# A warm-up of the matmul engine, later diagonals, and the last attention slot of the first batch turned by blocks, in a fused threshold attention and MLP kernel

## The chip, the cores and the metric

The kernel runs on one core of one Trainium2 chip. The metric is the device time of the whole kernel in microseconds (us). Before the change it took 1442.96 us, the median of three runs (1442.68 to 1445.76). The profile shown here is of one execution, whose span is 1443.0 us.

## The reference

Two blocks follow one another. The first is an attention with a threshold, for batch 8, 8 heads, 576 positions and head width 64; the second is a layer norm, a two-layer MLP with a residual, of width 512 and hidden width 2048.

```python
scores = (q @ k.T) / 8                       # per batch and head: 576 x 576
thresh = max(scores, axis=-1) - tau
scores = where(scores >= thresh, scores, -1e9)
attn = exp(scores - max(scores)); attn = attn / (sum(attn) + 1e-9)
x = attn @ v                                 # heads side by side: (8, 576, 512)
xn = (x - mean(x)) / sqrt(var(x) + 1e-6) * g_ln
out = x + relu(xn @ w_ch1) @ w_ch2
```

All inputs are float32 but the two weight matrices, which arrive as float64; the kernel converts them itself.

## The kernel before, in words

**Slots.** The attention is cut into 72 slots, nine for each of the eight batches; n counts all slots from 0, s is the slot within its batch. A slot handles a pair of heads (a unit) with 256 of its query rows: slots s = 0 to 3 take the first 256 rows of the four pairs, s = 5 to 8 the next 256, and s = 4 takes what is left over of all four. The loop over the slots is lines 749 to 811. A slot runs: score products on PE (line 384), row maxima on DVE (398) and thresholds on POOL (402), exponentials on ACT (409), masking and row sums on DVE (416), the reciprocal of the sums (420). The weights then have to be turned (transposed) before they can be multiplied by v.

**Two ways to turn the weights.** In batch 0 (slots n = 0 to 8) the turn is done on PE: ACT makes four diagonal matrices that hold the reciprocals (427), and in the next slot PE multiplies each 128 x 128 piece of the weights by a diagonal (lines 453, 468; recorded as line 100 tile `tp`, and line 468 tile `tr`); ACT copies the results out of PSUM into `em` and `rest` (462, 477). From batch 1 on the turn is done by blocks: POOL scales the weights by the reciprocals (429), DVE transposes 32 x 32 blocks into a tile `et` (494), four transfers write `et` to a scratch `scr` in DRAM (500), and in the next slot two transfers read it back in the turned order into `em` and `rest` (509, 510). For this way the queries must have been turned in another order of columns, which `by_blocks` also decides (338). In both ways the product with v (538) of slot n is issued in the last quarter of slot n + 1 once the first batch's early slots are past.

**MLP steps between.** A group is half a batch (288 tokens), 16 groups in all. A generator (`ffn_steps`, 632) yields the MLP's products one at a time, and `second_part` (702) places a number of them in each of four quarters of a slot. The first layer's product for one of 16 hidden blocks is 16 PE instructions (each float32 product is two halves and is run in two passes), then ACT applies the relu (649) into `hidden`. The second layer's are 64 PE instructions for each of four output blocks; DVE multiplies the result by the inverse deviation (596) and POOL adds x (597), DVE transposes (602), and four transfers store it. PSUM gives two buffers (tag `ff`) to all of these, so a product waits for the reader of the product two before it.

**Weight conversion.** The weights come in 32 chunks of 512 KB (16 of the first layer, then 16 of the second). `fetch` (229) issues a transfer on the SP queue into a free room; rooms are lent by `w2_sb`, `hidden`, `et`, an x buffer and a staging tile, each up to a given chunk (211 to 215). At a later `tick` (306) a chunk is begun (DVE 263 and 267, ACT 271 and 275), carried (POOL 281), masked (DVE 290), and for the first layer scaled by `g_ln` (ACT 303). `fetch` stands at two places of a slot (762 and 802). The last chunks are converted in slots n = 8 and 9.

**What orders the work.** Every engine and the SP queue run their instructions in the order in which the program writes them: `manual_schedule` is set, and no scheduler moves anything. SP issues nearly all transfers, and a transfer whose wait is not met holds up all behind it. In the built program the transfers take eight semaphores in rotation, so the issue of one also waits until the transfer eight before it has landed. `load_qk` (102) loads queries and keys of the next unit as soon as the turn of the present one (321) has freed their single buffers. `run(n, i)` (691) runs what was put off to quarter i of slot n (i = -1: right after the scores).

Of the kernel before, what the change touches and what calls it, by code (L numbers as in the profile page):

```python
# [18 lines left out]
def kernel(  # L19
# [31 lines left out]
    nc = tc.nc  # L51
# [72 lines left out]
    def load_v(u):  # L124
# [9 lines left out]
        values_in[u] = (vt, vr)  # L134

    ctx.enter_context(tc.manual_schedule())
    nc.sync.dma_start(
        out=tau_sb, in_=bass.AP(tensor=tau.tensor, offset=tau.offset, ap=[[0, 128], [1, 1]])
    )
# [6 lines left out]
    load_v(0)  # L146
    make_identity(nc, ident)
    nc.vector.memset(eps_sb, 1e-6)
    nc.vector.memset(avg_sb, 1.0 / DM)

# [13 lines left out]
    class Weights:  # L166
# [13 lines left out]
        def __init__(self):  # L180
            self.chunks = [
                (w1_sb[i][:, c : c + WC], w_ch1[i * 128 : (i + 1) * 128, c : c + WC], i)
                for c in range(0, DF, WC)
                for i in range(NK)
            ] + [
                (
                    w2_sb[:, m, d : d + 4].rearrange("p d c -> p (d c)"),
                    w_ch2[d * 128 : (d + 4) * 128, m * 128 : (m + 1) * 128].rearrange(
                        "(d p) c -> p d c", p=128
                    ),  # L190
                    None,
                )
                for m in range(NK)
                for d in range(0, ND, 4)
            ]
            self.n1 = NK * (DF // WC)
            self.fetched = self.begun = self.carried = self.masked = self.ended = 0
            self.raw, self.made, self.due, self.ticks = {}, {}, [], 2
            flat = lambda t: t.rearrange("p a b -> p (a b)")

            x_room = ffn.tile([128, NK, TOK], F32, tag="x", bufs=3, name="x_room")
            stage = consts.tile([128, 8, WC], F32, name="stage")
            et = att.tile([128, NB, 128], F32, tag="et", bufs=1, name="et0")

            n1 = self.n1
            self.free = []
            for t, n, before in (  # L210
                (w2_sb.rearrange("p m d c -> p (m d) c"), ND // 2, lambda p: n1 + 2 * p),
                (hidden, 4, lambda p: 10),
                (et, 2, lambda p: 2 * n1),
                (x_room, 1, lambda p: 2 * n1),
                (stage, 4, lambda p: 2 * n1),
            ):
                for p in range(n):
                    self.free.append((before(p), -1, flat(t)[:, p * 2 * WC : (p + 1) * 2 * WC]))
# [95 lines left out]
            if self.begun < self.fetched:  # L314
                self.begin()

    def by_blocks(u):

        return units[u][0] > 0

    def turn(u):

        q_in, k_in = loaded.pop(u)
        qT = att.tile([128, 2, QH], F32, tag="qT", bufs=4, name="qT")
        kT = att.tile([128, S], F32, tag="kT", bufs=4, name="kT")  # L330
        ql = q_last[u % HP]
        nc.gpsimd.tensor_scalar(
            out=q_in, in0=q_in, scalar1=scl_sb, scalar2=1.0, op0=ALU.mult, op1=ALU.mult
        )
        nc.vector.transpose(kT, k_in.rearrange("p n c -> p (n c)"))
        for s in range(2):
            part = q_in[:, 9 * s : 9 * s + 8]
            if by_blocks(u):
                nc.vector.transpose(
                    qT[:, s].rearrange("p (j a c) -> p a j c", j=2, a=4),  # L340
                    part.rearrange("p (a j) c -> p a j c", j=2),
                )
            else:
                nc.vector.transpose(qT[:, s], part.rearrange("p n c -> p (n c)"))  # L344
        nc.vector.transpose(
            ql.rearrange("p (t c) -> p t c", t=2),
            q_in.rearrange("p (t n) c -> p t n c", t=2)[:, :, 8],
        )
        turned[u] = (qT, kT, ql)
# [61 lines left out]
    def weights(es, thr, divide):  # L411
# [6 lines left out]
                op0=ALU.is_ge, op1=ALU.mult, accum_out=den[:, i : i + 1],  # L418
            )
        nc.vector.reciprocal(den, den)  # L420
        diags = []
        for i in range(4):
            if not divide:
                if i % 2 == 0:
                    two = ffn.tile([128, TOK], F32, tag="o", bufs=6, name="diag")
                diags.append(two[:, i % 2 * 128 : i % 2 * 128 + 128])
                nc.scalar.mul(diags[i], ident, den[:, i : i + 1])
                continue
            nc.gpsimd.tensor_scalar(  # L429
                out=es[:, i], in0=es[:, i], scalar1=den[:, i : i + 1], scalar2=1.0,  # L430
                op0=ALU.mult, op1=ALU.mult,
            )
        return diags


# [255 lines left out]
    def run(n, i):  # L691
        for fn, args in later_calls.pop((n, i), ()):
            fn(*args)
# [55 lines left out]
    for n in range(NS):  # L749
# [8 lines left out]
        run(n, -1)  # L758
        rest = exponentials()
        es, thr = next(rest)  # L760
        run(n, 0)
        conversion.fetch(2)
        run_all(stores)
        second_part(n, 0)
        next(rest, None)
# [8 lines left out]
        run(n, 1)  # L774
        second_part(n, 1)
        tick(2)
        blocks_go = by_blocks(b * HP)
        diags = weights(es, thr, blocks_go)
        run_all(aside)
        run_all(stores)  # L780
        tick(3)
        run(n, 2)
        second_part(n, 2)
        tick(4)
        box = []
        if blocks_go:
# [12 lines left out]
        if s in (HP, 2 * HP):  # L799
            group_ready(2 * b + (s > HP))  # L800
        run_all(aside)
        conversion.fetch(2)
        tick(5)
        run(n, 3)
        if b == 0 and s < HP - 2:
# [43 lines left out]
```

## Time and profile before

| What | us |
|---|---|
| span | 1443.0 |
| PE busy | 1389.0 (96%) |
| DVE busy | 871.8 (60%) |
| ACT busy | 422.2 (29%) |
| POOL busy | 439.1 (30%) |
| PE busy in the first 100 us | 68.4 |
| PE busy in 100 to 200 us | 92.8 |
| PE busy in 300 to 1400 us | 1091.8 of 1100 |

The page's second part shows the busy tenths of each engine in 40 slices of 36 us; the third row of interest is the granted PE clock. Its fourth part is the chain of work that ended last. The timeline of an engine lists its instructions in order of time, merged where alike: start, duration, engine, line, operation, tile written and tiles read, and in brackets the idle time before and what ended it. Times are counted from the start of the span. A slot is found in it by its score products (line 384) on PE: n = 0 at 10.0 us, n = 1 at 21.5, n = 6 at 87.4, n = 7 at 119.9, n = 8 at 142.2, n = 9 at 164.6, n = 10 at 191.6, n = 11 at 212.0.

### The profile page before, as it was taken

Reading aid. Unit: us, or ns where it says so; the run is one execution under the profiler, and the core shown is the slowest. Engines: PE = TensorE matmul, PEld = TensorE weight load, DVE = VectorE, ACT = ScalarE, POOL = GpSimd, SP = SyncE. Lnnn points to the kernel's source line nnn. Section 1 sums busy time; section 2 is a strip of 40 time slices with the busy share of each in tenths; the row PEclk is TensorE's granted clock in tenths of the full one; section 3 lists DMA queues with packets and bytes.
Section 4 is the critical chain, followed back from the end, with each engine's and each line's share of the span. In section 5 each row is a group of like instructions: output and inputs, shape, how many; then the busy total and the mean of one; then the engine's idle time right before and its main releaser. Section 6 shows DMA issues by size and latency. Waiting matters only on the chain.

```text
span 1443.0 us, 29649 instructions
## 1 busy us (share of the span) xinstructions
PE 1389.0 (96%) x12168; PEld 859.7 (60%) x12168; DVE 871.8 (60%) x1492; ACT 422.2 (29%) x818; POOL 439.1 (30%) x681
## 2 busy tenths in 40 slices
PE   5879999999999999999999999999999999999998
PEld 3655666655556565655556555565556555565664
DVE  5998857556565666566655565556665566656111
ACT  3887513132221313132221312223132322213020
POOL 2444332333323233232322333232332323222100
PEclk8999999999999999999999999999999999999999
DMA  9622466657845677557855577555775578555301
GB/s 226 168 73 83 90 137 157 172 148 162 176 133 145 148 173 173 145 131 171 183 150 145 146 160 167 140 144 143 176 167 143 136 170 185 139 144 137 79 6 17
DMA packets 466840, 205.12 MB, mean 142 GB/s; under 512 B 275024, under 2 KB 428368, under 8 KB 466704
## 3 DMA queue, kind: packets, MB, share of 16 engines
q1 hardware_dynamic: 461936, 202.64, 58.4%
q8 instruction: 95, 1.56, 0.5%
q10 hardware_dynamic: 4736, 0.59, 0.4%
q14 instruction: 41, 0.34, 0.1%
q0 software_dynamic: 32, 0.00, 0.0%
HBM read 119.41 MB, written 83.76 MB: 141 GB/s over the span
## 4 chain that ended last, share of the span: by engine, by line
PE 85%; DVE 4%; DMA 4%; SPq 3%; ACT 2%; issue 1%; POOL 0%; POOLq 0%; DVEq 0%; ACTq 0%
PE p L100 64%; PE sc L538 10%; PE sc L384 9%; SPq L115 2%; DMA em<-scr 1%; DVE e L416 1%; PE tp L100 1%; DVE neg L398 1%; DMA v_in<-in_v_dram 1%; ACT e L409 1%; DMA rest<-scr 0%; DMA scr<-et 0%; PE mean L100 0%; DVE w L263 0%; SPq L500 0%
## 5 line engine op out<-in xcount | busy, mean ns | idle before, releaser
L100 PE MATMUL p<-xc,w 128*64 128x288 f32 x4096 | 515.2, 407 | 7.4 <-ACT hidden L649 5.9
L100 PE MATMUL p<-hidden,w 128*64 128x288 f32 x4096 | 513.7, 407 | 0.0
L100 PEld LDWEIGHTS p<-xc,w 128*64 128x64 f32 x4096 | 294.9, 137 | 211.9 <-ACT hidden L649 12.6
L100 PEld LDWEIGHTS p<-hidden,w 128*64 128x64 f32 x4096 | 297.9, 137 | 196.5 <-issue 9.3
L398 DVE TENSOR_REDUCE neg<-sc 128x2 f32<-128x1152 f32 x144 | 188.7, 1352 | 252.2 <-PE sc L384 252.2
L409 ACT ACTIVATE e<-sc,neg 128x576 f32<-128x576 f32 x288 | 194.5, 742 | 296.5 <-DVE neg L398 290.1
L429 POOL TENSOR_SCALAR e<-e,den 128x576 f32<-128x576 f32 x252 | 187.9, 763 | 239.6 <-DVE den L420 239.5
L416 DVE SCALAR_TENSOR_TENSOR e<-sc,thr,e 128x576 f32<-128x576 f32 x288 | 219.0, 810 | 23.7 <-ACT e L409 23.7
L494 DVE STREAM_TRANSPOSE et<-e 128x1152 f32<-128x1152 f32 x112 | 153.6, 1375 | 77.3 <-POOL e L429 57.1
L649 ACT ACTIVATE hidden<-p 128x288 f32<-128x288 f32 x256 | 105.7, 413 | 292.0 <-PE p L100 290.6
L384 PE MATMUL sc<-kT,qT 64*128 64x384 f32 (+3 forms) x1024 | 150.6, 425 | 20.0 <-DVE qT L344 10.0
L402 POOL TENSOR_SCALAR thr<-neg,low_sb 128x2 f32<-128x2 f32 x144 | 41.6, 289 | 387.4 <-DVE neg L398 382.5
L384 PEld LDWEIGHTS sc<-kT,qT 64*128 64x128 f32 x1024 | 94.2, 191 | 77.5 <-issue 27.0
L538 PE MATMUL sc<-em,v_in 128*64 128x256 f32 (+1 forms) x1408 | 131.3, 330 | 6.0 <-DMA em<-scr 2.2
L538 PEld LDWEIGHTS sc<-em,v_in 128*64 128x64 f32 x1408 | 86.9, 137 | 45.8 <-DVE et L494 7.0
L555 ACT COPY x<-sc 128x256 f32<-128x256 f32 x60 | 22.4, 373 | 286.4 <-PE sc L538 284.4
L596 DVE TENSOR_TENSOR o<-p,rb 128x288 f32<-128x288 f32 x64 | 28.4, 443 | 127.9 <-PE p L100 127.9
L597 POOL TENSOR_TENSOR o<-o,x 128x288 f32<-128x288 f32 x64 | 51.0, 797 | 115.4 <-DVE o L596 114.0
L564 POOL TENSOR_TENSOR sum<-sum,x 128x256 f32<-128x256 f32 (+1 forms) x64 | 32.8, 512 | 97.6 <-ACT x L555 95.1
L655 POOL TENSOR_TENSOR sq<-sq 128x288 f32<-128x288 f32 x48 | 38.8, 808 | 44.0 <-ACT sq L653 41.5
L538 PE MATMUL sc<-rest,v_rest 128*64 128x256 f32 (+1 forms) x352 | 44.7, 329 | 0.0
L100 PE MATMUL tp<-diag,e 128*64 128x128 f32 x576 | 35.5, 278 | 6.6 <-ACT em L462 5.3
(130 smaller groups left out, 701.2 us busy)
## 6 DMA issues: line engine op xcount, KB each, us to landing
scr<-et SPq DMA_DIRECT2D x252, 288.0 KB, 4.6
em<-scr SPq DMA_DIRECT2D x63, 1024.0 KB, 5.9
out_dram<-ot SPq DMA_DIRECT2D x256, 36.0 KB, 4.4
q_in<-in_q_dram SPq DMA_DIRECT2D x124, 72.0 KB, 3.8
k_in<-in_k_dram SPq DMA_DIRECT2D x120, 72.0 KB, 2.8
v_in<-in_v_dram SPq DMA_DIRECT2D x64, 128.0 KB, 4.4
rest<-scr SPq DMA_DIRECT2D x63, 128.0 KB, 6.0
w<-in_moe_w_ch_dram SPq DMA_DIRECT2D x10, 512.0 KB, 6.0
```

What stands on the lines that cost most here:

```text
L100: nc.tensor.matmul(out[r], lhsT=lhsT[:, r], rhs=rhs, **flags)
L384: nc.tensor.matmul(sc[h][64 * i : 64 * i + 64 if s == HP else 128, at : at + n], lhsT=ql[r] if s == HP else qT[r, half, j * 128 : (j + 1) ...
L398: nc.vector.tensor_reduce(out=neg[:, i], in_=pairs[h], axis=AXL.X, op=ALU.max, negate=True,)
L402: nc.gpsimd.tensor_scalar(out=thr[:, i], in0=neg[:, i], scalar1=-1.0, scalar2=low_sb, op0=ALU.mult, op1=ALU.add,)
L409: nc.scalar.activation(es[:, i], blocks[i], func=AF.Exp, bias=neg[:, i : i + 1])
L416: nc.vector.scalar_tensor_tensor(out=es[:, i], in0=blocks[i], scalar=thr[:, i : i + 1], in1=es[:, i], op0=ALU.is_ge, op1=ALU.mult, accum_o ...
L429: nc.gpsimd.tensor_scalar(out=es[:, i], in0=es[:, i], scalar1=den[:, i : i + 1], scalar2=1.0, op0=ALU.mult, op1=ALU.mult,)
L494: nc.vector.transpose(et[:, :, 64 * h : 64 * h + 64].rearrange("p n (j c) -> p j n c", j=2), es[:, 2 * h : 2 * h + 2].rearrange("p j (n c) ...
L538: nc.tensor.matmul(dst[64 * h : 64 * h + 64], lhsT=vt[:, c, h, :] if c < J else vr[:, h, :], rhs=pick(em[:, c] if c < J else er, hp, h), s ...
L597: nc.gpsimd.tensor_tensor(out=o, in0=o, in1=groups[g][:, m], op=ALU.add)
L649: nc.scalar.activation(hidden[:, d], p1, func=AF.Relu)
L655: nc.gpsimd.tensor_tensor(out=sq[:, 0], in0=sq[:, 0], in1=sq[:, c], op=ALU.add)
```

## The change

Four edits are made together.

1. **Warm-up.** The tile `avg_sb`, a constant, is filled first of all on DVE, and PE runs 20 products of it with itself (40 halves of 128 columns) into a PSUM tile that nobody reads, before the first scores. This is to have the PE clock up when the first scores come.
2. **Diagonals later.** For slots n = 5, 6 and 7 the four diagonals on ACT are made after the third quarter's MLP steps, and not before them. This is to keep them out of the way of the relu.
3. **Slot n = 8 by blocks.** The last slot of batch 0 is turned by blocks and not on PE; the second half of the queries of unit 3 is turned accordingly. This takes the 32 halves into `tp` and the 4 products into `tr` off PE. The `et` tile is lent to the conversion only up to chunk 26 (before: 31), so that it is free for this.
4. **Fetches ahead.** Both calls of `fetch` are moved up in the slot, so that chunk transfers stand on the SP queue ahead of the transfers of turned weights: the first before `run(n, 0)`, which reads `scr` back, the second before `turn_blocks`, which writes it.

```diff
+    nc.vector.memset(avg_sb, 1.0 / DM)
+    warm = ps_ff.tile([128, 128], F32, tag="ff", name="warm")
+    for _ in range(20):
+        product(warm, lhsT=avg_sb, rhs=avg_sb, start=True, stop=True)
     nc.sync.dma_start(
...
-                (et, 2, lambda p: 2 * n1),
+                (et, 2, lambda p: 2 * n1 - 5),
...
-    def by_blocks(u):
-        return units[u][0] > 0
+    def by_blocks(n):
+        return n >= 2 * HP
...
-            if by_blocks(u):
+            if by_blocks(SLOTS * (u // HP) + u % HP + s * (HP + 1)):
...
+    def diagonals(den):
+        diags = []
+        for i in range(4):
+            if i % 2 == 0:
+                two = ffn.tile([128, TOK], F32, tag="o", bufs=6, name="diag")
+            diags.append(two[:, i % 2 * 128 : i % 2 * 128 + 128])
+            nc.scalar.mul(diags[i], ident, den[:, i : i + 1])
         return diags
...
         es, thr = next(rest)
+        conversion.fetch(2)
         run(n, 0)
-        conversion.fetch(2)
         run_all(stores)
...
-        blocks_go = by_blocks(b * HP)
-        diags = weights(es, thr, blocks_go)
+        blocks_go = by_blocks(n)
+        den = weights(es, thr, blocks_go)
+        if n <= HP:
+            diags = diagonals(den)
         run_all(aside)
         run_all(stores)
         tick(3)
         run(n, 2)
         second_part(n, 2)
+        if HP < n < 2 * HP:
+            diags = diagonals(den)
+        conversion.fetch(2)
         tick(4)
...
         run_all(aside)
-        conversion.fetch(2)
         tick(5)
```

In the built program the order on PE is the same as before but for the 40 added halves at the start and the 36 of slot 8 (32 into `tp`, 4 into `tr`) that are gone. Beside the turn itself, the other engines' order differs in the conversion: which rooms the chunks use, and when the last ones are fetched and begun. Before, chunks 27 and 28 (counted from 0) are fetched by the first call in slot 8, 29 and 30 by the second, and 31 by the first in slot 9. After, chunk 27 is fetched by the first call in slot 8, 28 and 29 by the second, right ahead of slot 8's `scr` transfers, chunk 30 by the first call in slot 9, right ahead of the read of `scr`, and chunk 31 by the second in slot 9, behind that read, the next query and key loads and four stores. On DVE chunk 28 is begun right ahead of the transposes into `et` of slot 8, and chunk 31 right ahead of those of slot 9. One chunk's mask (290) moves from slot 9 to slot 10, ahead of the subtraction of the mean (579) there.

## Prediction

> **What bounds the kernel now.** I first read the busy tenths. PE is full from about 115 us on, and only before that is there anything to win by waiting less; DVE is full in the slices before.
>
> ```profile
> PE   5879999999999999999999999999999999999998
> DVE  5998857556565666566655565556665566656111
> PEclk8999999999999999999999999999999999999999
> PE 85%; DVE 4%; DMA 4%; SPq 3%; ACT 2%; issue 1%; POOL 0%; POOLq 0%; DVEq 0%; ACTq 0%
> ```
>
> The last line is the chain that ended last: 85% of it is PE. So time is gained in two ways: PE instructions taken out once PE is full, and the first 115 us made shorter. Then I read the timelines around each edit. The start, PE, then DVE, then the SP queue:
>
> ```profile
> 10.04 4.21 PE L384 MATMUL sc<-kT,qT 64*128 64x384 f32 x16 [10.04 <-DVE qT L344]
> 21.50 5.68 PE L384 MATMUL sc<-kT,qT 64*128 64x384 f32 x16 [7.24 <-DVE e L416]
> ...
> 41.03 0.78 DVE L335 STREAM_TRANSPOSE kT<-k_in 128x576 f32<-128x576 f32 x1
> ...
> 33.80 4.79 SPq L115 DMA_DIRECT2D k_in<-in_k_dram  x4
> ```
>
> The first scores take 4.21 us, in slot 7 and later 2.21 for the same 16 instructions. The keys of unit 3 are issued until 38.6 and turned at 41.03. Slot 6, PE and ACT:
>
> ```profile
> 111.73 1.68 PE L100 MATMUL p<-xc,w 128*64 128x288 f32 x12 [2.76 <-ACT hidden L649]
> ...
> 108.39 1.28 ACT L427 ACTIVATE diag<-ident,den 128x128 f32<-128x128 f32 x4
> 109.56 0.72 ACT L303 ACTIVATE w<-w,g_sb 128x512 f32<-128x512 f32 x1
> 111.27 0.70 ACT L649 ACTIVATE hidden<-p 128x288 f32<-128x288 f32 x2
> ```
>
> PE waits 2.76 us for a relu, and ACT, busy without a gap, has the diagonals ahead of it. The turn of slot 8 on PE, and the place where PE next leans on DVE:
>
> ```profile
> 166.76 1.09 PE L100 MATMUL tp<-diag,e 128*64 128x128 f32 x16
> 174.80 11.80 PE L100 MATMUL p<-hidden,w 128*64 128x288 f32 x95
> 203.91 2.16 PE L100 MATMUL p<-xc,w 128*64 128x288 f32 x16 [0.73 <-DVE o L596]
> ...
> 193.91 2.62 DVE L398 TENSOR_REDUCE neg<-sc 128x2 f32<-128x1152 f32 x2 [2.70 <-PE sc L384]
> ...
> 185.61 3.74 SPq L500 DMA_DIRECT2D scr<-et  x4
> 193.93 0.41 SPq L509 DMA_DIRECT2D em<-scr  x1
> ```
>
> The turn costs 174.80 - 166.76 = 8.04 us, of it some 3.5 waiting for ACT's copies. From the write of `scr` to the issue of its read pass 8.32 us.
>
> [...]
>
> **Part 1, warm-up.** [...] DMA is full (the table by stretches gives it shares of 1.02, 1.00 and 0.97 in 10 to 20, 20 to 40 and 40 to 60 us), and unit 3's keys must land before the turn at 41.03. Their issue ends at 38.6, and landing takes 2.4 to 3.1 us from issue by the page's group of transfers: 41.0 to 41.7, or a little earlier for the pieces issued before. So that turn has no slack on its transfers. Earlier turns of units 1 and 2 free the buffers earlier, but an issue also waits for the transfer eight before it, and those are paced by bandwidth. I take 0.8 (0.4 for the POOL and DMA wait behind it and 0.4 for the landing); bounds 0 and 2.0. After that DVE is full until slot 6 and passes on what it got.
>
> **Part 2, diagonals.** In slot 6 the relu comes 1.19 us earlier (the group takes 1.28, starts 1.17 ahead of the next), so PE gains 1.2. The diagonals then lie behind the relu; ACT ends that stretch at 115.6 as before, and the next relu at 116.10 still comes before PE needs it (111.73 - 1.2 = 110.5, then 12 passes, the values' 2.2 and 20 passes: 116.6). In slot 5 no MLP runs, in slot 7 PE did not wait for the relu: 0, hidden behind ACT's conversion and behind 5.74 us of products. Bounds 0 and 1.2; I take 1.2.
>
> **Part 3 and 4, slot 8.** Times in this part are those of before (all is shifted by parts 1 and 2 alike). PE loses 8.04 us of work after 166.8. POOL gains 2.9 (four scalings, as at 203.70), ACT loses its copies; both have room. But DVE and SP get a new order.
> - DVE in slot 8 has one chunk less ahead of the masking, so the masking ends near 158.3 and not 160.3. Then it must begin chunk 28, whose transfer is issued at 157.97 (behind the key loads) and lands 4.0 us later, at 162.0: DVE waits. `et` of slot 8 is then made from 163.1 to 165.9 (2.74).
> - `scr` is written from 165.9; its read is issued 8.3 us later at 174.2 and lands 6.0 later (the group of `em` transfers), at 180.2. PE wants it at 186.28 - 8.04 = 178.2: PE waits 2.0.
> - Chunk 30, issued behind the `scr` writes and the values near 172.2, lands near 176.8; DVE waits for it ahead of slot 9's masking, which ends at 181.6 and not 179.95. This costs PE nothing: the scores of slot 10, which need that PSUM, come at 185.
> - Chunk 31 stands behind the read, the loads of unit 6 and a store. The third key load is the eighth transfer after the read, so it waits for 180.2; two key loads (1.2) and four stores (2.0) later, near 183.5, chunk 31 is issued and lands 4.0 to 5.0 us later, at 188.0.
> - DVE begins chunk 31 ahead of `et` of slot 9. Queued behind it are: that `et` (so slot 9's own turn), a store's transpose, the release of a PSUM buffer (596) for which PE's mean waits, and the maxima of slot 10. From 188.0: 1.1 + 2.75 + 0.43 + 0.45, and the maxima start at 192.7, not at 193.91. From there to the release that PE awaits at 203.91 pass 10.0 us, plus 0.68 for the mask that moved into slot 10: 203.4. And slot 9's `et`, done at 191.85, has its `em` landed at 191.85 + 8.3 + 6.0 = 206.2, where PE wants it at 205.9.
> So of the 8.04 us nothing is left at 206: +0.3 to +0.4. The gain is turned into a wait for the last chunk. Behind 206 PE is full and keeps what shift there is.
>
> Sum: -0.8 - 1.2 + 0.4 = -1.6, from 1442.96: 1441.4.
>
> **Rivals.**
> - *The turn pays.* The last chunks land in time, or DVE's wait lies in slack: PE loses 8.04, waits 2.0 for slot 8's `em`, and pays 0.7 for the moved mask: -5.3. With -0.8 and -1.2: -7.3, 1435.7. For it: chunk transfers waited hardly ever before (0.35 us at 163.56). Against it: they were issued a slot earlier then, and chunk 31 needs 181 for this, when SP still holds the key loads back.
> - *The wait costs more than the turn.* Chunk 30's 512 KB ahead of `em` delays it by 1.7 (512 KB at some 300 GB/s, a fast slice of the DMA row between 140 and 240 us), chunk 31 needs 5.0, and line 263 takes 1.5 and not 0.4, as it does beside POOL at 144.43: 190.7 + 1.1, so +4.2; and with nothing from parts 1 and 2 (the relu meets the next wait), 1447.2. For it: each is seen in the trace. Against it: all must come together.
> - *The start pays in full*: 2.0 from the warm-up, all else as forecast: -2.8, 1440.2; its chance is part of my forecast's.
>
> **How the numbers follow.** Chances: my forecast 0.50 (of it 0.08 below 1440.1), the turn pays 0.32, it costs more 0.18. 0.2% is 2.9 us: faster is below 1440.1, slower above 1445.8. So faster 0.40, same 0.42, slower 0.18. The range reaches to both rivals: 1435 to 1447.
>
> **What would show it.** Slot 0's scores in 2.2 us and slot 1's still slow; unit 3's keys turned at 40 to 41; the relu wait in slot 6 at 1.6; no `tp` rows in slot 9; DVE idle some 2 us in slot 8, and 3 and 5 in slot 9, ahead of the first step of a chunk (line 267 after), for a weight transfer; PE waiting for `em` and for the PSUM release (line 603 after). I am wrong if the DVE waits for chunks 28, 30 and 31 are missing (then 1436), or if unit 3's keys land 2 us earlier.

## The result and the profile after

The changed kernel takes 1458.82 us (median of 6 runs, 1452.38 to 1463.99); the kernel before, run beside it, 1445.18 us. The ratio is 1.0092 with a 95% interval of 1.0064 to 1.0121: it is slower by 13.6 us. The forecast was 1441.4 us, with a range of 1435 to 1447: it was wrong in size and in sign.

The busy tenths and the chain that ended last, from the page of the changed kernel:

```profile
PE   6879989999999999999999999999999999999998
DVE  5899756566665666656665565656665566655211
PEclk8999999999999999999999999999999999999999
PE 78%; DVE 6%; DMA 6%; SPq 4%; ACT 2%; issue 2%; POOL 1%; POOLq 0%; DVEq 0%; ACTq 0%
```

PE's row has an 8 in the sixth slice (182 to 219 us), where before it had nines, and PE's share of the chain fell from 85% to 78%. DMA, DVE and SP took its place. To see where that happened, put the starts of the slots (first score products on PE) of both traces side by side, after minus before in us:

| slot | 1 | 2 | 3 | 6 | 7 | 8 | 9 | 10 | 11 | 12 | 18 | 36 | 71 |
|---|---|---|---|---|---|---|---|---|---|---|---|---|---|
| shift | -2.0 | -0.6 | +1.9 | +1.4 | -0.2 | -0.4 | -0.4 | +0.7 | +4.9 | +9.7 | +9.5 | +11.5 | +15.9 |

There are two losses: 4 us between slots 1 and 3, and 10 us in slots 9 to 11. (Behind slot 12 a trace drifts by some us, here down to +9.5 in slot 18 and up to +15.9 in slot 71, as single reads of `em` come late, by up to 2.7 us, and single stretches run at a slower clock, here 3.41 us at half clock from 902.74; the medians of the runs decide, the shifts only say where.)

**The start**, the timelines of PE and of DVE, and below them the turn of unit 2's keys in the kernel before:

```profile
1.06 6.51 PE L100 MATMUL warm<-avg_sb 128*64 128x128 f32 x80 [1.06 <-DVE eps_sb L153]
10.04 2.21 PE L388 MATMUL sc<-kT,qT 64*128 64x384 f32 x16 [2.47 <-DVE qT L348]
19.49 5.68 PE L388 MATMUL sc<-kT,qT 64*128 64x384 f32 x16 [7.24 <-DVE e L420]
...
30.31 0.78 DVE L339 STREAM_TRANSPOSE kT<-k_in 128x576 f32<-128x576 f32 x1 [3.31 <-DMA k_in<-in_k_dram]
43.73 0.78 DVE L339 STREAM_TRANSPOSE kT<-k_in 128x576 f32<-128x576 f32 x1 [1.73 <-DMA k_in<-in_k_dram]
```

```profile
28.92 0.77 DVE L335 STREAM_TRANSPOSE kT<-k_in 128x576 f32<-128x576 f32 x1
```

The warm-up does what it is for: slot 0's scores take 2.21 us, slot 1 starts 2 us early. But DVE then waits 3.31 us for the keys of unit 2, which before were there at 28.92, where DVE did not wait for them, and turns those of unit 3 at 43.73, not 41.03. The keys themselves come later than before: their last pieces land at 30.18 and 43.61, before at 28.32 and 40.91.

**Slot 6**, PE and ACT:

```profile
111.56 1.68 PE L100 MATMUL p<-xc,w 128*64 128x288 f32 x12 [1.59 <-ACT hidden L656]
...
111.10 0.70 ACT L656 ACTIVATE hidden<-p 128x288 f32<-128x288 f32 x2
111.68 1.29 ACT L439 ACTIVATE diag<-ident,den 128x128 f32<-128x128 f32 x4
```

The diagonals now lie behind the relu, and PE's wait for it fell from 2.76 to 1.59 us.

**Slots 8 to 11**, PE first, then DVE and ACT:

```profile
181.37 2.59 PE L545 MATMUL sc<-em,v_in 128*64 128x256 f32 x16 [3.10 <-DMA em<-scr]
192.33 3.82 PE L388 MATMUL sc<-kT,qT 64*128 64x384 f32 x16 [3.98 <-ACT x L562]
210.72 1.95 PE L545 MATMUL sc<-em,v_in 128*64 128x256 f32 x16 [2.08 <-DMA em<-scr]
230.79 3.38 PE L545 MATMUL sc<-em,v_in 128*64 128x256 f32 x16 [3.28 <-DVE et L501]
...
161.15 0.43 DVE L267 TENSOR_SCALAR stage<-w 128x512 uint32<-128x512 uint32 x1 [1.82 <-DMA w<-in_moe_w_ch_dram]
177.29 0.43 DVE L267 TENSOR_SCALAR stage<-x_room 128x512 uint32<-128x512 uint32 x1 [5.12 <-DMA x_room<-in_moe_w_ch_dram]
190.71 0.43 DVE L267 TENSOR_SCALAR stage<-stage 128x512 uint32<-128x512 uint32 x1 [7.56 <-DMA stage<-in_moe_w_ch_dram]
191.78 2.63 DVE L501 STREAM_TRANSPOSE et<-e 128x1152 f32<-128x1152 f32 x2
...
190.79 0.68 ACT L275 ACTIVATE stage<-stage 128x512 int32<-128x512 uint32 x1 [12.25 <-DMA stage<-in_moe_w_ch_dram]
191.93 0.34 ACT L562 COPY x<-sc 128x256 f32<-128x256 f32 x1
```

No `tp` products stand in slot 9 any more, but PE waits four times for 2 us or more. The three DVE waits for chunks 28, 30 and 31 are there. Two things the prediction didn't have: chunk 31 stops ACT too, and behind it on ACT stands the copy of slot 8's values, which frees the PSUM that the scores of slot 10 need (3.98 us); and a wait in slot 11 (3.28). SP's queue shows where the last one comes from:

```profile
186.64 0.40 SPq L247 DMA_DIRECT2D stage<-in_moe_w_ch_dram  x1
194.44 3.81 SPq L507 DMA_DIRECT2D scr<-et  x4
202.76 0.45 SPq L516 DMA_DIRECT2D em<-scr  x1
206.56 4.90 SPq L115 DMA_DIRECT2D q_in<-in_q_dram  x4
215.75 3.89 SPq L507 DMA_DIRECT2D scr<-et  x4
```

Slot 10's `et` is complete at 210.9, but SP issues its `scr` only at 215.75. Ahead of it stand the queries, whose issue takes 4.90 us since its third piece, the eighth transfer after the read of slot 9's `em` (issued 202.76, landed 210.59), is issued only at 210.60, then keys and a store. One late `em` delays the next.

The scores of slot 10 and the products with `em` in slots 9 and 11 are also slow (3.82 us against 2.21, 2.59 and 3.38 against 1.95 in slot 10). The table by stretches gives the granted clock (PEclk, 1.00 is full speed):

```profile
core 0: us, PE busy (x) PEld busy (x) DVE busy (x) ACT busy (x) POOL busy (x), PEclk, DMA share, GB/s
188.00:192.00 4.00, 0.34 (x4) 0.00 (x0) 1.26 (x3) 1.21 (x3) 0.01 (x1) 1.00 0.44 127
192.00:196.00 4.00, 3.67 (x16) 2.30 (x16) 3.11 (x4) 0.27 (x2) 2.77 (x3) 0.60 0.13 31
```

PE idles for nearly 4 us, and in the 4 us after that the clock is at 0.60 in the mean. Stretches at half clock also begin at 182.5 and 230.3 us, at the waits of 3.10 and 3.28 us. So these three waits are paid for twice.

### The profile page after: what moved, and what is told of

Its sections match the earlier page's. It is cut to its first block, busy times and chain, and to the rows that moved or that the text cites. A ratio compares the mean times of both kernels' runs of the same rounds, so it can differ in the third digit from the quotient of the medians.

```text
span 1458.6 us, 29670 instructions
## 1 busy us (share of the span) xinstructions
PE 1397.4 (96%) x12176; PEld 857.4 (59%) x12176; DVE 871.6 (60%) x1494; ACT 417.1 (29%) x809; POOL 441.7 (30%) x685
## 4 chain that ended last, share of the span: by engine, by line
PE 78%; DVE 6%; DMA 6%; SPq 4%; ACT 2%; issue 2%; POOL 1%; POOLq 0%; DVEq 0%; ACTq 0%
PE p L100 58%; PE sc L545 10%; PE sc L388 9%; DMA em<-scr 2%; SPq L115 2%; DVE e L420 1%; DVE neg L402 1%; DMA v_in<-in_v_dram 1%; SPq L507 1%; DVE et L501 1%; ACT e L413 1%; DMA scr<-et 1%; POOL e L426 1%; SPq L133 1%; SPq L129 1%
## 5 line engine op out<-in xcount | busy, mean ns | idle before, releaser
L100 PEld LDWEIGHTS p<-hidden,w 128*64 128x64 f32 x4096 | 293.2, 137 | 203.1 <-issue 10.5
L426 POOL TENSOR_SCALAR e<-e,den 128x576 f32<-128x576 f32 x256 | 191.3, 764 | 244.3 <-DVE den L424 244.3
L545 PE MATMUL sc<-em,v_in 128*64 128x256 f32 (+1 forms) x1408 | 134.8, 336 | 18.1 <-DMA em<-scr 11.1
L545 PEld LDWEIGHTS sc<-em,v_in 128*64 128x64 f32 x1408 | 88.2, 139 | 60.4 <-DVE et L501 11.8
L603 DVE TENSOR_TENSOR o<-p,rb 128x288 f32<-128x288 f32 x64 | 28.3, 442 | 125.1 <-PE p L100 125.1
L571 POOL TENSOR_TENSOR sum<-x 128x256 f32<-128x256 f32 (+1 forms) x32 | 17.0, 532 | 86.5 <-ACT x L562 54.9
```

The lines of the kernel that those rows point to most:

```text
L100: nc.tensor.matmul(out[r], lhsT=lhsT[:, r], rhs=rhs, **flags)
L426: nc.gpsimd.tensor_scalar(out=es[:, i], in0=es[:, i], scalar1=den[:, i : i + 1], scalar2=1.0, op0=ALU.mult, op1=ALU.mult,)
L545: nc.tensor.matmul(dst[64 * h : 64 * h + 64], lhsT=vt[:, c, h, :] if c < J else vr[:, h, :], rhs=pick(em[:, c] if c < J else er, hp, h), s ...
L571: nc.gpsimd.tensor_tensor(out=sums[g][:, cols], in0=x[:, 0, cols] if c == 1 else sums[g][:, cols], in1=x[:, c, cols], op=ALU.add,)
```

## The experiments

In all of them times are medians, the kernel before run beside them, and shifts are slot starts against the trace of before.

### One part at a time

Part 1 alone:

```diff
+    nc.vector.memset(avg_sb, 1.0 / DM)
+    warm = ps_ff.tile([128, 128], F32, tag="ff", name="warm")
+    for _ in range(20):
+        product(warm, lhsT=avg_sb, rhs=avg_sb, start=True, stop=True)
...
-    nc.vector.memset(avg_sb, 1.0 / DM)
```

> The kernel before with the warm-up alone. Theory (the loss comes from slot 8 by blocks, whose shorter loan of et delays the last weight chunks): the time stays within 2 us of the kernel before; slot 0's scores take 2.2 us, and slots 2 to 6 shift by -1 to +2 us, as the keys of units 2 and 3 land. Rival (the start carries the loss: a disturbed stream of transfers at the start shifts everything): +1.4 us at slot 5 and more than +5 us at the end.

Measured: 1448.63 against 1444.33 us, ratio 1.0032 (1.0016 to 1.0047). The warm-up alone costs 4.3 us. Shifts: -1.9 in slot 1, +1.1 in slot 3, +2.9 in slots 4 to 6, +4.6 in slot 7. Unit 2's and unit 3's keys keep DVE waiting 2.71 and 3.57 us. What comes between slots 6 and 7 is told further below.

Part 2 alone (slots 5 to 7; slot 8 keeps its diagonals early):

```diff
-        diags = weights(es, thr, blocks_go)
+        den = weights(es, thr, blocks_go)
+        if n <= HP or n == 2 * HP:
+            diags = diagonals(den)
...
         second_part(n, 2)
+        if HP < n < 2 * HP:
+            diags = diagonals(den)
```

> The kernel before with the diagonals of slots 5 to 7 made after the third quarter's MLP steps, alone. Theory: the relu wait in slot 6 falls from 2.76 to 1.6 us, slot 7's scores come 1.2 us earlier and the end too: -1.2 us, ratio 0.999. Rival (the diagonals later hold up the turn in the next slot): no gain, or slower by 1 us.

Measured: 1443.05 against 1444.33 us, ratio 0.9987 (0.9980 to 0.9995). It gains 1.3 us; slot 7 stands at -1.1, slots 8 to 12 at -1.0 to -1.3. The prediction's term was -1.2.

Part 3 alone, with the fetches in their old places (behind the transfers of turned weights):

```diff
-        return units[u][0] > 0
+        return n >= 2 * HP
...
-                (et, 2, lambda p: 2 * n1),
+                (et, 2, lambda p: 2 * n1 - 5),
```

> The kernel before with slot 8 by blocks and et lent up to chunk 26 only; both fetches at their old places. Theory: slower by 6 to 14 us, with DVE waiting for the last chunks in slots 9 and 10 and PE waiting for em; here the chunks stand behind the scr writes, so not less than in the whole change. Rival (moving the fetches makes the loss): within 2 us, or faster by up to 7 us, as 36 halves are gone from PE.

Measured: 1467.8 against 1444.33 us, ratio 1.0155 (1.0132 to 1.0178). The diagonals of slots 5 to 7 stay early here, as before. The timeline of PE at the start of slots 9 and 10 of this kernel:

```profile
175.98 4.21 PE L384 MATMUL sc<-kT,qT 64*128 64x384 f32 x16 [11.33 <-ACT x L558]
206.64 4.21 PE L384 MATMUL sc<-kT,qT 64*128 64x384 f32 x16 [8.86 <-ACT x L558]
```

Twice ACT's copy is stuck behind a chunk, for 11.3 and 8.9 us: the two chunk transfers in question were issued behind `scr`, at 167.5 and 198.0 us, and landed late, at 174.4 and 205.1.

Part 4 alone:

```diff
         es, thr = next(rest)
+        conversion.fetch(2)
         run(n, 0)
-        conversion.fetch(2)
...
+        conversion.fetch(2)
         tick(4)
...
         run_all(aside)
-        conversion.fetch(2)
         tick(5)
```

> The kernel before with both fetches moved up alone, slot 8 still turned on PE. Theory: within 1 us; no scr transfers stand in slots 8 that chunks could pass, and all rooms are there. Rival (moving the fetches makes the loss): slower by 5 us or more, with SP holding the loads of queries and keys behind a fetch that waits for its room.

Measured: 1445.58 against 1444.33 us, ratio 1.0005 (0.9997 to 1.0012): no difference. With no turn by blocks in slot 8 there is no transfer of turned weights to get ahead of.

Parts 2, 3 and 4 together, the warm-up left out:

```diff
-    for _ in range(20):
-        product(warm, lhsT=avg_sb, rhs=avg_sb, start=True, stop=True)
```

> The whole change without its first part: diagonals later, slot 8 by blocks, fetches moved; the mean's constants set where they were before. Theory (parts add up): the warm-up costs here what it costs alone, 4.3 us, so some 1454 us, with slots 1 to 8 at or ahead of the kernel before and slot 12 at about +8. Rival (the start is swallowed): slots 10 and 11 wait for chunk 31 and for SP's queue, whose times follow from transfers and not from the start, so the total stays within 1 us of the whole change, 1458.

Measured: 1454.56 against 1445.49 us, ratio 1.0064 (1.0043 to 1.0084): 9.1 us over before, the whole change 13.6 over it. So the warm-up costs 4.6 us here by the medians, 4.3 alone. That these agree so well is in part chance: the two intervals reach 4 and 3 us to either side, and in the traces the whole change lies only 2.1 us behind this kernel at slot 4, 2.3 at slot 12 and 5.1 at slot 71. But the 2 us of the start are still there behind slots 10 and 11, so the rival (these slots swallow the start) falls. Slots 3 to 8 stand at -0.5 to -2.3, slot 12 at +7.4. With the diagonals' 1.3 taken off, blocks and fetches together cost 10.4 us, blocks alone 23.5: part 4 is worth 13 us once part 3 is there.

### Why the warm-up costs time

With the warm-up, transfers land as before up to 13.0 us, and then late: those that landed at 13.3 and 13.5 us come at 14.6 and 14.7, unit 2's keys at 29.1 instead of 28.3, unit 3's at 42.9 instead of 40.9. What is new at that time is one packet. The transfers between 8 and 16 us by queue (packets, MB, share of the DMA engines' time), of the kernel with the warm-up alone:

```profile
q1 hardware_dynamic: 3063, 1.40, 86.8%
q10 hardware_dynamic: 1404, 0.17, 23.3%
q8 instruction: 1, 0.02, 1.0%
```

Before has no line for q8 there. The packet is 16384 bytes, starts at 11.84 us and takes 1.27 us; in the kernel before the first such packet starts at 35.66, when PE has begun 252 matmuls and weight loads. In the whole change it starts at 11.80, when PE has begun 190, 160 of them the warm-up's. The page after has 95 packets on q8, and PE's matmuls and weight loads are 2 x 12176 = 24352, 256.3 for each packet; the warm-up alone has 96 packets for 24496, the blocks alone 95 for 24192. So the packets on q8, which the profile calls instruction, go with the number of PE's instructions, and 80 passes with their 80 weight loads bring the first one forward into the first loads, where the shares above add up to more than the whole of the DMA engines' time. Whether that makes the keys late, or the earlier slots do, three runs tell.

As many instructions, less TensorE time (the 80 passes took 4.44 us, with the warm-up alone 7.06):

```diff
-        product(warm, lhsT=avg_sb, rhs=avg_sb, start=True, stop=True)
+        product(warm[:, :8], lhsT=avg_sb, rhs=avg_sb[:, :8], start=True, stop=True)
```

> The kernel before with the 80 passes of the warm-up cut to 8 columns each: as many instructions, hardly any TensorE time, so that slot 0's scores stay slow (4.2 us) and slots 0 and 1 are where they were. Theory (instruction fetch): the first 16 KB of instructions come near 12 us again, transfers from 13 us on land 1 to 2 us later, DVE waits for unit 2's keys although nothing runs earlier, slot 3 starts 1 to 3 us later, total 2 to 5 us over before. Rival (the gain of the first slots turns against itself): landings and slots 0 to 5 as before, total within 1 us.

Measured: 1450.09 against 1444.66 us, ratio 1.0048 (1.0029 to 1.0067). Slots 0 to 2 start within 0.1 us of before and are as slow; the packet comes at 11.80 us and takes 1.25; what landed at 13.3 us lands at 14.5; unit 2's keys land at 30.1, unit 3's at 44.0; slot 3 starts 2.3, slot 4 4.2 us late. Nothing ran earlier, so the instructions alone are enough to make the keys late. Of the 5.4 us, 4.1 are there at slot 6; 1.7 more come between slots 6 and 7. DVE's turn of unit 3's keys:

```profile
44.16 0.78 DVE L339 STREAM_TRANSPOSE kT<-k_in 128x576 f32<-128x576 f32 x1 [3.17 <-DMA k_in<-in_k_dram]
```

How the delay grows from 1.2 us to 3 on the way to these keys isn't told apart: an issue also waits for the transfer eight before it, and the second packet on q8 comes early as well, at 39.52 instead of 48.38, when the keys are on their way. SP's queue shows the first delay in the four `hidden` issues, here and, below, in the kernel before:

```profile
11.35 3.04 SPq L247 DMA_DIRECT2D hidden<-in_moe_w_ch_dram  x4
```

```profile
11.37 2.01 SPq L243 DMA_DIRECT2D hidden<-in_moe_w_ch_dram  x4
```

Ten products over 512 columns of constants, `ones` (half the instructions of the 80 passes):

```diff
-    for _ in range(20):
-        product(warm, lhsT=avg_sb, rhs=avg_sb, start=True, stop=True)
+    for _ in range(10):
+        product(warm, lhsT=avg_sb, rhs=ones, start=True, stop=True)
```

> The kernel before with a warm-up of the same length but a quarter of the instructions: ten products over 512 columns of constants (20 matmul passes) instead of twenty over 128 (80 passes). Theory (instruction fetch): the 80 passes bring PE's first fetch of 16 KB of instructions forward from 35.7 to 11.8 us, into the full transfers of the first loads; with 20 passes it comes after 25 us, keys of units 2 and 3 land as in the kernel before (28.3 and 40.9), and the total is 1441 to 1444. Rival (earlier first slots send the loads into each other, or PE's clock is charged for the warm-up): keys of unit 3 land 2 us late as with the 80 passes, and the total is 1447 to 1450.

Measured: 1444.08 against 1445.49 us, ratio 0.9996 (0.9985 to 1.0006). It came out as 40 passes and 11.55 us, twice what was meant, so slot 0 started 3.0 us late. Still the first packet came at 32.29, unit 2's keys were turned without a wait at 29.96, and by slot 3 only +0.4 was left: a start 3 us late cost less than an early packet.

Five such products:

```diff
-    for _ in range(10):
+    for _ in range(5):
```

> The kernel before with a short warm-up of few instructions: five products over 512 columns of constants (20 matmul passes, some 6 us) instead of twenty over 128 (80 passes). Theory (instruction fetch): slot 0's scores take 2.2 us and slot 1 starts some 2 us early as with the 80 passes, PE's first 16 KB of instructions come after 30 us and not at 11.8, unit 2's keys are turned without a wait (28 to 29 us), unit 3's by 41.5, and the total is 0 to 2 us under before. Rival (an earlier slot 1 itself makes the keys late, or idling after the warm-up does): unit 2's and 3's keys wait 2.7 and 3.6 us as with the 80 passes and the total is 3 to 5 us over before.

Measured: 1448.87 against 1444.66 us, ratio 1.0026 (1.0012 to 1.0041). Half of the theory held: the packet came at 30.72, slot 0's scores took 2.21, slot 1 started at -2.0, slot 2 at -2.8, and the keys landed as before or earlier (27.9, 40.9). So an earlier start alone didn't make the keys late here. But unit 3's keys came no earlier either, so the gain was gone by slot 4 (+0.3), as the prediction's landing bound had it; and the total is 4 us over, as the rival said, though not by the way it named. In that trace 1.7 us come between slots 6 and 7 and 3.7 between slots 42 and 48. The first have a cause that can be read. The table by stretches, edges laid on the clock's own changes, of this kernel and of the kernel before:

```profile
109.70:113.11 3.41, 1.08 (x10) 0.69 (x12) 1.94 (x2) 3.41 (x8) 3.41 (x4) 1.00 0.22 71
113.11:116.52 3.41, 3.41 (x20) 1.81 (x17) 3.38 (x4) 2.65 (x5) 2.26 (x2) 0.50 0.47 142
```

```profile
110.02:113.43 3.41, 1.70 (x14) 1.06 (x16) 2.58 (x2) 3.41 (x8) 3.41 (x3) 1.00 0.42 116
113.43:116.85 3.42, 3.42 (x32) 2.15 (x30) 3.37 (x4) 2.87 (x6) 1.97 (x2) 1.00 0.48 148
```

Both kernels wait the same 2.76 us for the relu in slot 6. Before, PE was busy for 1.70 us of that stretch of 3.41, and the clock stayed; here the wait lies otherwise to the stretches, PE was busy for 1.08, and the next 3.41 us ran at half. Where the stretches lie isn't set by the kernel: the clock changes at 28.11 us in the trace of before and at 111.82 in that of the fetches alone, which starts in the same way, and these are 24.5 stretches apart, while within a trace all changes lie whole stretches apart. So whether a wait meets a bad place is the chance of an execution, and one trace doesn't say how often it does in the others. The warm-up alone (half clock at 115.4 to 118.8), the ones with narrow and with ten wide products and the fetches alone (111.8 to 115.2) show the same; the whole change, whose wait is 1.59, doesn't. What the 3.7 us at slot 42 are besides one more such stretch (894.8 to 898.2) is left open, and with it what the five wide products cost in the median: their six runs go from 1445.5 to 1450.2 us, and the one in the trace is among the slowest.

### Which wait costs what in slots 8 to 11

All of these but one leave the warm-up out, so they are compared with 1454.56 us, the time without it. A fifth room for the conversion, so that chunks 30 and 31 are fetched together, ahead of slot 8's `em`:

```diff
-            stage = consts.tile([128, 8, WC], F32, name="stage")
+            stage = consts.tile([128, 10, WC], F32, name="stage")
...
-                (stage, 4, lambda p: 2 * n1),
+                (stage, 5, lambda p: 2 * n1),
...
-            rb = ffn.tile([128, TOK], F32, tag="rb", bufs=2, name="rb")
+            rb = ffn.tile([128, TOK], F32, tag="rb", bufs=1, name="rb")
```

> The same with a fifth room of two chunk halves for the conversion (stage 10 wide instead of 8; the MLP's root takes one buffer instead of two to make place), so that chunks 30 and 31 are fetched ahead of slot 8's em instead of one before and one some 10 us after. Theory (the last chunk comes late): DVE's wait near 190 goes, ACT's copy for slot 10's scores is not held up, slot 9's et is ready some 7 us earlier; slot 12 stands at 0 to +2 against before although em of slot 8 comes up to 3 us later; total 1442 to 1446. Rival (the round trip through DRAM itself is the cost): em of slot 8 late by 3 us more, slots 11 and 12 still over +6, total 1452 or more.

Measured: 1448.1 against 1445.49 us, ratio 1.0018 (1.0006 to 1.0029): 6.5 us better than without. ACT's copy no longer holds up slot 10, slot 11 stands at -3.0. But `em` of slot 8 is awaited for 5.83 us, and in slot 11 the queries ahead of `scr` cost 3.36 us on PE as they did before the mend: slot 12 is at +2.2. Both answers were partly right.

The block turn ahead of the chunk on DVE:

```diff
+        late = n in (2 * HP, 2 * HP + 1)
+        if not late:
+            tick(4)
-        tick(4)
...
             at_quarter(n + 1, 0, lambda s=s, scr=scr, box=box: box.append(fetch(s, scr)))
+            if late:
+                tick(4)
```

> The whole change without the first part, and in slots 8 and 9 the fourth tick of the conversion (begin of a chunk among it) comes after the block turn on DVE, not ahead of it; transfers in the same order as before. Theory (et behind the chunk): et of slot 9 is ready near 184 instead of 193.5, so em of slot 9 is in time, SP issues the scr of slot 10 some 5 us earlier and slot 11 loses no 4.8 us; ACT's copy behind chunk 31 still costs slot 10 its 4 us: slot 12 near +3, total 1447 to 1450. Rival (the copy and the late chunk decide, et doesn't): slot 12 within 1.5 us of the kernel with the order unchanged.

Measured: 1445.08 against 1445.49 us, ratio 1.0004 (0.9988 to 1.0019): 9.5 us better, better than expected. PE's timeline in slots 9 and 10:

```profile
178.05 1.95 PE L541 MATMUL sc<-em,v_in 128*64 128x256 f32 x16 [2.10 <-DMA em<-scr]
188.14 4.21 PE L384 MATMUL sc<-kT,qT 64*128 64x384 f32 x16 [4.81 <-ACT x L558]
203.05 2.16 PE L100 MATMUL p<-xc,w 128*64 128x288 f32 x16 [0.51 <-ACT hidden L652]
```

The waits for `em` of slots 9 and 10 are gone. `et` of slot 9 is made from 179.96, in the whole change from 191.78, and SP issues the `scr` of slot 10 at 207.12, right when its `et` is complete (204.27 + 2.82 = 207.1). The copy on ACT still costs 4.81 us and the clock after it. Slot 12: -0.9.

Both mends, with `em` read ahead of the two chunks:

```diff
         es, thr = next(rest)
-        conversion.fetch(2)
         run(n, 0)
+        conversion.fetch(2)
```

> Slot 8 by blocks with both mends: fifth room for the conversion, fourth tick behind the block turn in slots 8 and 9, and em of slot 8 read ahead of the chunks (this fetch back in its old place); diagonals later, no warm-up. Theory (late chunks and what stands behind them were the whole loss): PE waits at most 3 us for em of slot 8, no wait of DVE above 4 us for a chunk, no 4.8 us wait of slot 10's scores for ACT's copy, scr of slot 10 issued as soon as its et is made; slot 12 at -4 to -7, total 1438 to 1441. Rival (the round trip of slots 8 to 11 binds in SP's order): slot 12 no better than -1, total 1444 or more.

Measured: 1449.66 against 1444.66 us, ratio 1.0043 (1.0026 to 1.0059), where the theory had 1438 to 1441. The timeline of DVE shows why:

```profile
181.42 0.43 DVE L263 TENSOR_SCALAR stage<-stage 128x512 uint32<-128x512 uint32 x1 [9.46 <-DMA stage<-in_moe_w_ch_dram]
```

Chunk 30, now behind `em`, landed at 181.4 (177.3 in the whole change); DVE begins it ahead of slot 9's masks and waited 9.46 us, and PE waited as long for the PSUM that the masks release. Here part 4's order is the right one.

The same with the five wide warm-up products:

> The same with the five wide warm-up products. Theory (the start's gain survives if no instructions are fetched into the loads): 0.5 to 2 us less than without, 1437 to 1440. Rival (transfers pace slots 2 to 5 anyway): the same within 0.5 us, or up to 1 us more.

Measured: 1451.43 against 1444.66 us, ratio 1.0041 (1.0025 to 1.0057). Slot 2 is at -2.5 and slot 3 at +2.5: unit 3's keys, for which DVE waits 5.32 us, land at 43.9. Why isn't shown: PE's first packet comes at 29.98, not early, and SP issues as many transfers ahead of these keys as in the kernel with the five wide products alone, where they landed at 40.9. So early instructions are not the only thing that can make these keys late. The start's gain wasn't to be had in this way.

Both mends, chunks ahead of `em` as in the change:

> Whole change without the warm-up, with a fifth room for the conversion and the fourth tick behind the block turn in slots 8 and 9; both late chunks still fetched ahead of em of slot 8. Theory (each mend takes away another wait): masks of slot 9 near 175, no wait of slot 10's scores for ACT's copy, em of slot 8 waited for 4 to 6 us on PE since 1 MB goes ahead of it, scr of slot 10 without delay; slot 12 at -2 to -4, total 1440 to 1443. Rival (the mends take away the same wait twice): slot 12 near -1 as with the turn first alone, total 1444 to 1446.

Measured: 1444.78 against 1445.25 us, ratio 0.9995 (0.9986 to 1.0004). Slot 10's scores no longer wait, `em` of slot 8 is awaited for 5.88 us as expected; slot 12 stands at -0.9. One wait was changed for another.

The next two were meant to put ACT's copy ahead of chunk 31 by moving slot 9's fourth tick behind `run(n, 3)`. They did not: the fifth tick, which stands ahead of the copy, begins the chunk instead, and ACT's order is unchanged. The second of them also has slot 9's masks ahead of its first two ticks and `em` of slot 8 ahead of chunk 30.

```diff
             if n == 2 * HP:
                 tick(4)
...
         run(n, 3)
+        if n == 2 * HP + 1:
+            tick(4)
```

> As the run with the turn first, and the fourth tick of slot 9 (begin of chunk 31) also behind the values' copy on ACT and a store's transpose on DVE; transfers in the same order. Theory (ACT's copy behind chunk 31 costs what its wait shows): the 4.8 us wait of slot 10's scores goes, PE stays fast there; slot 12 4 us ahead of the run with the turn first, near -5, total 1439 to 1442. Rival (PE then waits for em of slots 9 or 10 instead): the wait shows up as em on PE in slots 10 to 11, slot 12 near -1, total 1444 to 1446.

> As the run with the copy first, and in slot 9 also the first two ticks (begin of chunk 30 among them) behind the masks, and em of slot 8 read ahead of chunk 30. Theory (no wait of DVE holds work that PE needs): masks of slot 9 near 171, em of slot 8 waited for at most 1 us, slot 12 near -6, total 1438 to 1441. Rival (chunk 30 is needed by then): PE waits for its weights or for slot 9's em; no gain over the run with the copy first.

Measured: 1446.68 and 1444.86 against 1445.25 us, ratios 1.0011 (0.9999 to 1.0023) and 0.9997 (0.9984 to 1.0011). Slot 10's scores wait 3.16 and 4.79 us for the copy. No gain, and none due.

With the fifth tick moved too:

```diff
-        tick(5)
+        if n != 2 * HP + 1:
+            tick(5)
         run(n, 3)
+        if n == 2 * HP + 1:
+            tick(4)
+            tick(5)
```

> As the run with the turn first, and fourth and fifth tick of slot 9 behind the values' copy, so that on ACT the copy comes ahead of chunk 31. Theory (the wait is worth its size until the round trip binds): slot 10's scores start near 183.5 without a wait and take 2.2 us; slot 11 stands near -7; then em of slot 10, whose scr leaves SP no earlier than its et and the stores before it, is awaited for 2 to 3 us; slot 12 near -4 and total 1440 to 1442. Rival (the time is set by the round trips of slots 9 and 10): all of the gain goes into waits for em; slot 12 near -1 and total 1444 to 1446.

Measured: 1442.83 against 1445.07 us, ratio 0.9986 (0.9973 to 0.9999). Slot 10's scores don't wait and take 2.2 us (slot 10 stands at -8.0 and slot 8 at -2.5, so 5.5 of the turn's 8.0 us are kept). Then PE waits once for a weight that is masked later:

```profile
183.59 2.21 PE L384 MATMUL sc<-kT,qT 64*128 64x384 f32 x16
193.53 3.85 PE L100 MATMUL p<-hidden,w 128*64 128x288 f32 x16 [2.24 <-DVE w L290]
```

The theory had waits for `em` take some of it back; it was chunk 31 itself, begun later, with 2.24 us and a slow stretch after them. Slot 12: -4.2.

The same with slot 9's masks ahead of the first two ticks, and `em` of slot 8 read ahead of chunk 30:

```diff
-        tick(1)
+        behind = n == 2 * HP + 1
+        if not behind:
+            tick(1)
...
         den = weights(es, thr, blocks_go)
+        if behind:
+            tick(1)
+            tick(2)
```

> As the run before it, and slot 9's masks ahead of the first two ticks, em of slot 8 read ahead of chunk 30. Theory: 1 us less than the run before it (em of slot 8 is awaited 1.0 and not 2.1 us); slot 12 near -5, total 1439 to 1441. Rival (chunks are begun later and PE meets their weights): PE waits for a weight's mask or scaling in slot 9 or 10, total as the run before it or more.

Measured: 1442.28 against 1445.07 us, ratio 0.9980 (0.9967 to 0.9993). It is faster than both kernels, by 2.8 and by some 16 us. Of the 2.8, the diagonals give 1.3; the rest, by medians, is not clear of noise. Slot 10 stands at -9.8, slot 12 at -5.0; `em` of slot 8 isn't awaited.

The waits can be added up. For each kernel: PE's waits from slot 8 to 12 by its timeline; half of the time in which PE was busy at half clock, by the record of the clock ("slow clock"); the sum less 8.04 for the turn that is gone and 0.73 for a wait that before had there; and the shift measured between slots 8 and 12.

| kernel | waits | slow clock | sum - 8.77 | measured |
|---|---|---|---|---|
| whole change | 13.2 | 4.9 | +9.2 | +10.1 |
| without warm-up | 12.5 | 5.1 | +8.8 | +9.7 |
| fifth room | 9.7 | 4.0 | +4.9 | +5.3 |
| turn first | 7.4 | 2.9 | +1.6 | +1.8 |
| copy ahead | 4.9 | 1.7 | -2.1 | -1.6 |
| all ahead | 5.1 | 0 | -3.7 | -2.5 |

So what happens in these slots is accounted for within some 1 us, and of the 18.1 us that the whole change loses there against the turn's 8.0, 4.9 are the slow clock. For the blocks alone the sum is 4 us too high (+24.0 against +19.8), as there 36 passes of the MLP's, some 4 us, fall behind slot 12.

## Why the prediction was wrong

**Right:** the kind of each step in slots 6 to 9. The relu wait is 1.59 us (1.6 predicted), the diagonals alone gain 1.3 (1.2). Slot 0's scores take 2.21, slot 1's stay slow (5.68). DVE waits for exactly the chunks that were named (1.82, 5.12 and 7.56 us; some 2, 3 and 5 predicted). PE wanted slot 8's `em` at 181.37 - 3.10 = 178.3 (178.2). The rival named "the wait costs more than the turn" had the right side, with +4.2 for these slots at under half of the size, and no loss at the start. Its 190.7 for the begin of chunk 31 is the measured time by luck: it put the issue 1.7 us later than the forecast and the transfer at 5.0 us; the issue came 3.1 us later and the transfer took 4.1.

**Wrong, part 1:** "I take 0.8", with "bounds 0 and 2.0" on the gain. No run shows the 0.8: with the warm-up alone slot 1 started 1.9 us early, slot 3 1.1 us late, and the kernel lost 4.3, which was not within the bounds. The sum has no term for what the 80 passes cost. They are also 160 instructions, and with these a packet of 16384 bytes came at 11.84 us, when the DMA was full (86.8% and 23.3% of its engines' time from 8 to 16 us), and not at 35.66. In that kernel's trace 2.9 us stand at slot 4, with the late keys, and 1.7 come with the half clock after slot 6's wait. The remark that unit 3's keys have "no slack" was right, and should have been turned round: what has no slack can also be made late.

**Wrong, parts 3 and 4, a size:** chunk 31 was put at 188.0 and came at 190.7. Its issue was put near 183.5, which took `em` to land at 180.2; PE's wait for `em` ended at 181.37, the four key loads ended at 183.15 and the four stores took 3.30 us (put at 2.0), and that made it 186.64.

**Wrong, parts 3 and 4, a step left out:** "Queued behind it are ..." lists DVE's queue alone. The same chunk also heads ACT's queue, where the copy waits that frees slot 10's PSUM. This was 3.98 us of waiting. Putting the copy ahead is worth less, as chunk 31's own weights then come later: 3.2 us at slot 12 of the traces (-4.2 against -0.9 with the turn first alone), 1.8 by the medians, which is within their intervals.

**Wrong, the end of the sum:** "Behind 206 PE is full and keeps what shift there is." Slot 9's late `em` holds SP, which holds slot 10's `scr`; the whole change loses 4.9 us more in slot 11. In the run with the turn first this loss is gone.

**Left out: the clock.** The sum has no term for it behind the start. Three waits (3.10, 3.98 and 3.28 us) were each followed by a stretch of 3.41 us at half clock, 4.9 us in sum.

**One reading** was off, and nothing in the sum rests on it. The waits for ACT's copies in the turn of slot 8 are 4 x 0.69 = 2.8 us, not some 3.5.

The forecast's +0.4 for parts 3 and 4 is 10.4 by the runs, the -0.8 for part 1 is +4.3 to +4.6. The rival "the turn pays" is right of the turn, not of the change: when nothing that PE needs stands behind the late chunks it gains, 2.5 us from slot 8 to slot 12 of the last run's trace.

## What to carry to other kernels

A late transfer costs what stands behind its first reader on every engine that reads it, and then what stands behind those on the transfer queue: list all the queues, not only the nearest, and put the work that PE waits for ahead of the late transfer's readers. Here chunk 31 cost 3.98 us of PE's time behind ACT's copy, and slot 9's late `em` 4.9 in slot 11. Count the instructions of added work too: 160 more on an idle PE, whose passes were 8 columns wide, brought a packet of 16384 bytes into the first loads, where the DMA was full, and cost 5.4 us. When PE waits, look whether what follows runs at half clock: behind waits of 2.24 us (the copy ahead) and 3.98 us it did, behind one of 2.10 us (the turn first) it did not.

## What the runs showed of the hardware that was not expected

- One packet of 16384 bytes on q8 per 256.3 matmuls and weight loads of PE (24352 over 95 packets), 1.25 us for the packet at 11.8 us of the run with narrow products. In the first loads of that run what landed at 13.3 us before landed 1.2 us later, and unit 3's keys 3 us later.
- The clock halved after a wait shorter than a stretch: 2.76 us of 3.41 (the five wide products, in slot 6). The changes of the clock lie on multiples of 3.41 us from one another within a trace. A whole idle stretch was not needed: in all the traces, from 30 to 1395 us, every stretch at full clock with PE busy for 1.33 us of 3.41 or less was followed by one at half clock. One with 1.43 was followed by full clock (the diagonals alone, at 888.8 us), those of 1.47 to 1.51 by either, and one with 1.86 by half (the five wide products, at 44.8 us). So no sharp edge in PE's busy time is shown, and what else counts stays open. The same 2.76 us of waiting cost nothing in one trace and 1.7 us in another.
